# An HGRN2 attention block with a PReLU network behind it: increments as a stage of their own, other banks for two products, and a new order of the stages

## The chip, the cores and the metric

The kernel runs on one core of one Trainium2 chip. The metric is the time of one execution on the device in microseconds (us). A profiled execution has its own time, and its span runs from the first to the last recorded instruction.

## The reference

Four sequences of 768 tokens with eight heads of 48 channels go through a gated linear recurrence; the result, 3072 tokens of 384 channels, goes through a two-layer network with 2048 hidden channels. All is float32.

```python
f = 1.0 / (1.0 + np.exp(-f_logit))
for t in range(S):
    state = f[:, :, t, :, None] * state + np.einsum('bhd,bhe->bhde', k[:, :, t], v[:, :, t])
    y[:, :, t] = np.einsum('bhd,bhde->bhe', q[:, :, t], state)
# (B, H, S, D) -> (B * S, H * D) = x
h = x @ w_in
g = np.maximum(h, 0.0) + alpha * np.minimum(h, 0.0)
out = g @ w_out
```

## The kernel before

The sequence is cut into six chunks of 128 tokens (C), the batch into two pairs (U = 2), which gives twelve steps, `steps = [(bp, c) for c in range(NC) for bp in range(B // U)]`, numbered from zero here. Steps n and n + 2 belong to the same pair; the second needs the state that the first leaves. A chunk is cut into halves of 64 tokens (index `cc`) and blocks of 32 (DB). What is written below holds for steps 2 to 11; steps 0 and 1 have a start of their own.

Each step goes through stages, Python generators that yield between pieces. A piece is what is issued between two yields.

- P, `prepare`, 8 pieces: 1 the loads of f, q, k and v; 2 sigmoid and copies on ScalarE; 3 products of decays on VectorE; 4 copies on ScalarE and two scans; 5 to 7 scaled keys and queries on VectorE, among them `keys`, which ends with a 32x32 block transpose of the keys into `kt` (L422); 8 copies of scaled queries into A on ScalarE (L460).
- S and T, `scores` for u = 0 and 1, 4 pieces each: products of 32-token blocks on PE into `pairs[u]` (L579), masked copies into `ad` on VectorE (L588), products again, masked copies again (L598).
- K, `keys_moved`: 16 DMAs from `kt` to `ksn` that finish the transpose, eight issued by SP and eight by POOL (L470). M, `landed`: one ScalarE copy from `ksn` back into `kt` (L478).
- O, `carry`, 4 pieces: off products, between the two blocks of a half (PE, L511); their copies into A (ScalarE, L518); state increments, keys by values (PE, L542), which read `kt`; `moved(0)`, which decays the state and adds the first half's increments (VectorE, L552 and L556).
- Y, `attend`, 4 pieces: 1 and 2 copies of `ad` into A (ScalarE, L622); 3 the attention output, A by values and state (PE, L633); 4 its copies into `y` (ScalarE, L640), `moved(1)`, and ten DMAs from `y` to `xT`, spread over SP, ScalarE's and POOL's queues (L663). `y` and `ksn` share one buffer.
- n, `network`, 13 pieces. Pieces 1 to 8 are the first layer: each is six matmuls of 128x256 into a bank `ph` (L678), a negated relu on ScalarE (L683) and two VectorE operations into `gate` (L685); after the fourth and eighth, four VectorE sums into S (L764). The second layer is a 2x2 block product with seven block products instead of eight, each eight matmuls of 128x192 (L717): piece 9 is pa and pb, 10 pc and pd, 11 the second part of pa and of pc, 12 pe, three VectorE additions (L721) and the store of o1, 13 the last addition and the store of o0. pa, pc, pd and pe name the accumulators.
- a, w, b, g, W, i, j, X occur at the start only: weights, idle matmuls, and the handing over of banks.

On PE, VectorE, ScalarE and SP (SyncE, which only issues DMAs) instructions stand in the order in which the pieces are called; this order is a hand-held list, a start string and a round that repeats. A word `T:2` calls two pieces, a plus sign means the next step, and n runs for the step before:

```python
USUAL = "T:2 S:2 n:3 M n T:2 S n P+ S n P+ n:3 Y O P+ O:2 Y O n P+ Y:2 P+ n:3 P+:3 K+"
```

In round n the network of step n - 1 runs while scores, off products, increments and output of step n and the preparation of step n + 1 are set between its pieces.

PSUM has eight banks of 512 float32 columns. Four belong to `pairs` (two tiles of two banks): scores go to both, then off products and output to `pairs[0]`, increments to `pairs[1]`. The other four are handed to the network as a pool of four buffers, taken in turn by `bank`.

Of the kernel before, what the change touches and what calls it, by code (L numbers as in the profile page):

```python
# [8 lines left out]
F32 = mybir.dt.float32  # L9
# [5 lines left out]
AF = mybir.ActivationFunctionType  # L15
# [5 lines left out]

U = 2
CH = 64
NC2 = C // CH
# [4 lines left out]

BEGUN = 5  # L30
START = (
# [7 lines left out]
)  # L39
USUAL = "T:2 S:2 n:3 M n T:2 S n P+ S n P+ n:3 Y O P+ O:2 Y O n P+ Y:2 P+ n:3 P+:3 K+"  # L40

LOOSE = ("a", "w", "b", "g", "W", "i", "j", "X")

# [17 lines left out]
def kernel(  # L61
# [66 lines left out]
    def banks_of_network():  # L128

        early_ps.close()  # L130
        net["pool"] = ctx.enter_context(tc.tile_pool(name="psn", bufs=4, space=bass.MemoryType.PSUM))
        yield

    def bank(name):
        return net["pool"].tile([128, 512], F32, tag="net", name=name)

# [131 lines left out]
    def halves(cc):  # L268

        return slice(CH * cc, CH * cc + CH), slice(CH * (1 - cc), CH * (1 - cc) + D)  # L270

    def prepare(bp, c, x):

# [16 lines left out]

        for cc in range(NC2):
            t_, _ = halves(cc)
            loads.dma_start(out=vs[bp][t_, cc, :, 0:DM], in_=v[b0:b0 + U, c, t_].rearrange("u t d -> t u d"))
        yield
# [123 lines left out]
        def keys():  # L418
            nc.vector.tensor_tensor(ks[:, :, 0], kh, f32[:, 1:G:2].broadcast_to((128, GC, DB)), ALU.mult)
            if c:  # L420
                kt = x["kt"] = late["kt"].tile([128, W], F32, tag="kt", name=f"kt_{i}")
                nc.vector.transpose(kt, ks.rearrange("p g s t -> p (g s t)"))  # L422

# [38 lines left out]
        yield  # L462

    def keys_moved(bp, c, x):
        kt, i = x["kt"], f"{bp}_{c}"
        ksn = x["ksn"] = work.tile([128, U, HP * 128], F32, tag="ksn", name=f"ksn_{i}", bufs=1)
        for a in range(4):
            n = min(32, D - 32 * (a % 2))
            for b in range(NJ):
                (nc.gpsimd if a % 2 else nc.sync).dma_start(  # L470
                    out=ksn[32 * b:32 * (b + 1)].rearrange("p u (h x) -> p (u h) x", h=HP)[:, :, 32 * a:32 * a + n],
                    in_=kt[32 * a:32 * (a + 1)].rearrange("p (g b x) -> p g b x", b=NJ, x=32)[:, :, b, 0:n])
        yield
# [8 lines left out]
    def carry(bp, c, x):  # L482

        i = f"{bp}_{c}"
        home = more if (bp, c) == steps[0] else pairs
        off = home[0]
        if not c:
# [14 lines left out]
            yield  # L502
        q3, ks, kh, f64 = (x[n] for n in ("q3", "ks", "kh", "f64"))
        for u in range(U):
            for hp in range(HP):
                a = (u * HP + hp) * NC2
                h_ = slice(64 * (hp % 2), 64 * (hp % 2) + 2 * DB)
                o = (u * HP + hp) // 2 * 2 * DB
                for par in range(2):
                    r_ = rows(par)  # L510
                    nc.tensor.matmul(off[h_, par, o:o + 2 * DB], lhsT=kh[r_, a:a + 2].rearrange("p c s -> p (c s)"),  # L511
                                     rhs=q3[r_, a:a + 2, 2], start=True, stop=True)
        yield
        for cc in range(NC2):
            s_ = slice(CH * cc, CH * cc + DB)
            for e in range(2):
                of = off[64 * e + DB * cc:64 * e + DB * (cc + 1), :, 0:U * HP * DB]
                nc.scalar.copy(A[s_].rearrange("p u (r h e) t -> p r u h e t", r=2, e=2)[:, :, :, :, e, CH * cc + DB:CH * (cc + 1)],  # L518
                               of.rearrange("p r (u h c t) -> p r u h c t", u=U, h=HP // 2, c=NC2)[:, :, :, :, cc])

# [12 lines left out]
        yield  # L533
        pd = home[1]
        ksn = x["ksn"]
        for u in range(U):
            for hp in range(HP):
                for cc in range(NC2):
                    for par in range(2):
                        o = (u * HP + hp) * D  # L540
                        s_ = halves(cc)[0]
                        nc.tensor.matmul(pd[rows(par), cc, o:o + D],  # L542
                                         lhsT=ksn[s_, u, hp * 128 + 64 * par:hp * 128 + 64 * par + D],
                                         rhs=vs[bp][s_, cc, u, (2 * hp + par) * D:(2 * hp + par + 1) * D], start=True, stop=True)

        def moved(cc):
# [6 lines left out]
            for par in range(2):  # L553
                now = pd[rows(par), cc, 0:U * HP * D].rearrange("p (u h e) -> p u h e", u=U, e=D)
# [62 lines left out]
    def attend(bp, c, x):  # L617
# [7 lines left out]

        py = (more if (bp, c) == steps[0] else pairs)[0]
        for u in range(U):
            for hp in range(HP):
                for cc in range(NC2):
                    for par in range(2):  # L630
                        hd = 2 * hp + par
                        o = hp * C + CH * cc
                        nc.tensor.matmul(py[64 * par:64 * par + 64, u, o:o + CH],  # L633
                                         lhsT=vs[bp][:, cc, u, hd * D:hd * D + 64],
# [4 lines left out]
        for u in range(U):  # L639
            nc.scalar.copy(y[:, u].rearrange("p h t -> p (h t)"), py[:, u])  # L640
        if c < NC - 1:
            x["moved"](1)
        xT = x["T"] = work.tile([128, NK, T], F32, tag="xT", name=f"xT_{i}")
        if not (bp or c):

            yield
            for kt in range(NK):
                b = bank(f"xt{kt}_{i}")
                these = [hp for hp in range(HP) if 2 * D * hp < 128 * (kt + 1) and 2 * D * (hp + 1) > 128 * kt]
# [19 lines left out]
    def network(bp, c, x):  # L669
        i = f"{bp}_{c}"  # L670
        xT = x["T"]
        plain = (bp, c) == steps[0]
        for f in range(NH):
            ph = bank(f"ph{f}_{i}")
            tiles = (2 * f, 2 * f + 1) if plain else (f, f + NH)
# [19 lines left out]
        if plain:  # L695
            po = [bank(f"po{u}_{i}") for u in range(U)]
            for n, (f, u) in enumerate([(f, u) for f in range(NF) for u in range(U)]):
# [17 lines left out]
        def product(to, of, by, more=False):  # L715
            for f in range(NH):
                nc.tensor.matmul(to[:, 0:DH], lhsT=of(f), rhs=by(f), start=(f == 0 and not more), stop=(f == NH - 1),  # L717
                                 skip_group_check=True)

        def plus(to, of, by, scale=UP):  # L720
            nc.vector.scalar_tensor_tensor(to, of[:, 0:DH], scale, by, ALU.mult, ALU.add)  # L721

        o0, o1 = (work.tile([128, DM], F32, tag="o", name=f"o{u}_{i}") for u in range(U))
        kept, u2, u3 = (late["C"][:, n] for n in range(3))
        pa, pb = (bank(f"p{n}_{i}") for n in "ab")
        product(pa, a11, b11)
        product(pb, a22, t4)
        nc.scalar.activation(kept, pa[:, 0:DH], AF.Copy, scale=UP)
        yield
        pc, pd = (bank(f"p{n}_{i}") for n in "cd")  # L730
# [6 lines left out]
        plus(o0[:, DH:DM], pd, u2)  # L737
        nc.scalar.activation(o0[:, 0:DH], pa[:, 0:DH], AF.Copy, scale=UP)
        if (bp, c) == steps[-1]:
            store(0, o0, slice(0, DH))  # L740
        yield
        pe = bank(f"pe_{i}")
        product(pe, s4, b22)
# [22 lines left out]
    def halves_of_w_out():  # L766
# [4 lines left out]
        late["S"] = pool.tile([128, 4, NH, C], F32, tag="S", name="S")  # L771
        late["C"] = pool.tile([128, 3, DH], F32, tag="C", name="Csum")
        for n in ("t2", "t3", "t4"):
# [35 lines left out]
    with tc.manual_schedule(engines={mybir.EngineType.PE, mybir.EngineType.DVE, mybir.EngineType.Activation,  # L809
                                     mybir.EngineType.SP}):  # L810
        run = {}
        for n, step in enumerate(steps):
            x = {}
            for key, stage_ in zip("POYKMn", (prepare, carry, attend, keys_moved, landed, network)):
                run[key, n] = stage_(*step, x)
# [58 lines left out]
```

## Time and profile before

| | us |
|---|---|
| median of three runs | 603.27 |
| the three runs | 602.59 to 605.02 |
| the profiled execution | 602.63 |
| its span | 600.8 |
| TensorE clock granted, as a share of full speed | 1.00 |

PE is TensorE's matmuls, PEld its weight loads, DVE VectorE, ACT ScalarE, POOL GpSimd, SP SyncE; a q behind the name (SPq) means the queue of an engine's DMA issues. In groups of instructions `xT<-y` is output and input; L717 is a line of the kernel; `x352` a count. A float32 matmul shows as two instructions, so counts are twice the matmuls that are written. Behind the bar stand busy time in us and the mean of one in ns, then idle time of the engine before them and what ended it. In the chain of waits a row is start, length, work. In a timeline a row is start, length, engine, line, operation, with idle time before it in brackets.

### The profile page before, as it was taken

The numbers are of one execution on the slowest core, as the hardware profiler recorded it, in microseconds if no ns is written. First come the engines' busy times: TensorE is split into PE (matmuls) and PEld (weight loads), VectorE is DVE, ScalarE is ACT, GpSimd is POOL, SyncE is SP. The second block draws the span as 40 slices with busy tenths as digits, with TensorE's granted clock in tenths as the row PEclk, the third lists the DMA queues.
The fourth block names the chain that finished last, engine by engine and source line by source line (L and its number), as shares of the span: only waits on it lengthen the run. The fifth ranks groups of instructions, "written<-read, shape, count | busy, mean of one in ns | idle before, by whom it ended". The sixth has DMA issues, their size and how long they took to land.

```text
span 600.8 us, 18092 instructions
## 1 busy us (share of the span) xinstructions
PE 575.7 (96%) x7760; PEld 516.4 (86%) x7760; DVE 495.3 (82%) x998; ACT 246.6 (41%) x430; POOL 85.1 (14%) x162
## 2 busy tenths in 40 slices
PE   2489999999999999999999999999999999999997
PEld 1378667898899899899899889899899899899997
DVE  7989999997888769988997897997997997891351
ACT  5679951711452441550550451352343344232110
POOL 9210014013003003002100300300300300300000
PEclk9999999999999999999999999999999999999999
DMA  8778836025006303402501602601601511201000
GB/s 261 258 215 299 250 85 125 1 71 108 2 2 176 37 2 63 151 1 62 151 2 55 158 3 55 159 2 41 161 12 31 156 29 27 55 1 29 27 1 27
DMA packets 52880, 50.36 MB, mean 84 GB/s; under 512 B 26720, under 2 KB 43360, under 8 KB 52800
## 3 DMA queue, kind: packets, MB, share of 16 engines
q1 hardware_dynamic: 42784, 37.46, 22.3%
q0 software_dynamic: 5504, 9.90, 6.6%
q10 hardware_dynamic: 4512, 1.85, 1.3%
q8 instruction: 61, 1.00, 0.7%
q14 instruction: 19, 0.16, 0.1%
HBM read 36.21 MB, written 4.72 MB: 68 GB/s over the span
## 4 chain that ended last, share of the span: by engine, by line
PE 87%; DVE 8%; ACT 2%; POOL 1%; issue 1%; DVEq 0%; ACTq 0%; POOLq 0%
PE ph L678 39%; PE pc L717 10%; PE pa L717 10%; PE pair L579 6%; PE pe L717 5%; PE pd L717 5%; PE pb L717 5%; PE pair L633 3%; DVE gate L685 1%; PE pair L542 1%; DVE w_out_sb L248 1%; PE pair L511 1%; PE po L698 1%; DVE ad L598 1%; POOL mhalf L183 1%
## 5 line engine op out<-in xcount | busy, mean ns | idle before, releaser
L678 PE MATMUL ph<-xT,w_in_sb 128*128 128x256 f32 x1152 | 255.3, 381 | 0.6 <-DVE w_in_sb L248 0.6
L678 PEld LDWEIGHTS ph<-xT,w_in_sb 128*128 128x128 f32 x1152 | 216.9, 190 | 32.7 <-issue 2.2
L683 ACT ACTIVATE neg<-ph 128x512 f32<-128x512 f32 x96 | 56.1, 593 | 124.6 <-PE ph L678 81.1
L685 DVE SCALAR_TENSOR_TENSOR gate<-neg,om,ph 128x256 f32<-128x256 f32 x192 | 81.7, 478 | 27.9 <-ACT neg L683 27.8
L717 PE MATMUL pa<-w_out_sb,gate 128*128 128x192 f32 x352 | 62.7, 330 | 0.4 <-DVE gate L685 0.4
L717 PE MATMUL pc<-t,S 128*128 128x192 f32 x352 | 61.6, 328 | 0.0
L460 ACT COPY A<-q 48x512 f32<-48x512 f32 x44 | 27.1, 617 | 83.7 <-DVE q L408 83.2
L717 PEld LDWEIGHTS pa<-w_out_sb,gate 128*128 128x128 f32 x352 | 57.3, 190 | 2.4 <-DVE gate L685 1.0
L470 POOL DMA_DIRECT2D ksn<-kt x80 | 46.1, 584 | 85.6 <-DVE kt L422 61.4
L717 PEld LDWEIGHTS pc<-t,S 128*128 128x128 f32 x352 | 57.4, 190 | 0.4
L663 POOL DMA_DIRECT2D xT<-y x22 | 11.8, 543 | 289.2 <-ACT y L640 289.1
L598 DVE COPY_PREDICATED ad<-mquad,pair 128x224 f32<-128x224 int32 (+6 forms) x140 | 41.7, 298 | 4.1
L588 DVE COPY_PREDICATED ad<-mraw,pair 128x256 f32<-128x256 int32 (+1 forms) x96 | 41.2, 453 | 4.2 <-PE pair L579 0.9
L364 DVE TENSOR_TENSOR us<-us,fs 128x768 f32<-128x768 f32 (+5 forms) x60 | 36.9, 615 | 1.1
L764 DVE TENSOR_TENSOR S<-gate 128x512 f32<-128x512 f32 x44 | 30.2, 687 | 0.8
L717 PE MATMUL pe<-w_out_sb,S 128*128 128x192 f32 x176 | 30.5, 327 | 0.0
L717 PE MATMUL pb<-t,gate 128*128 128x192 f32 x176 | 30.4, 326 | 0.0
L717 PE MATMUL pd<-w_out_sb,S 128*128 128x192 f32 x176 | 30.4, 326 | 0.0
L552 DVE TENSOR_TENSOR vs<-vs,f 48x768 f32<-48x768 f32 x20 | 19.1, 953 | 13.4 <-PE pair L633 12.0
L622 ACT COPY A<-ad 32x512 f32<-32x512 f32 x48 | 29.4, 613 | 0.6
L640 ACT COPY y<-pair 128x512 f32<-128x512 f32 x22 | 11.8, 589 | 43.1 <-PE pair L633 43.1
L717 PEld LDWEIGHTS pe<-w_out_sb,S 128*128 128x128 f32 x176 | 28.8, 190 | 0.1
(125 smaller groups left out, 720.2 us busy)
## 6 DMA issues: line engine op xcount, KB each, us to landing
w_out_raw<-in_w_out SPq DMA_DIRECT2D x8, 767.8 KB, 6.7
w_in_raw<-in_w_in SPq DMA_DIRECT2D x8, 767.2 KB, 9.1
out<-o SPq DMA_DIRECT2D x23, 192.0 KB, 1.9
q<-in_qT SPq DMA_DIRECT2D x8, 512.0 KB, 5.1
k<-in_kT SPq DMA_DIRECT2D x8, 512.0 KB, 7.2
f<-in_fT SPq DMA_DIRECT2D x7, 512.0 KB, 4.0
vs<-in_v SPq DMA_DIRECT2D x16, 192.0 KB
ksn<-kt SPq DMA_DIRECT2D x80, 32.0 KB, 2.2
```

Of the source, the lines that this page charges most:

```text
L364: nc.vector.tensor_tensor(us[:, :, UO[m]:UO[m] + 4 * n].rearrange("p g (i r) -> p g i r", r=4), us[:, :, skip:skip + 4 * n].rearrange("p g ...
L460: nc.scalar.copy(A[halves(cc)[1], :, par * HP:(par + 1) * HP, CH * cc:CH * (cc + 1)], q3[rows(par)].rearrange("p (u h c) s t -> p u h c (s ...
L470: (nc.gpsimd if a % 2 else nc.sync).dma_start(out=ksn[32 * b:32 * (b + 1)].rearrange("p u (h x) -> p (u h) x", h=HP)[:, :, 32 * a:32 * a + n],
L579: nc.tensor.matmul(to[DB * j:DB * (j + 1), par, hp * step + lo:hp * step + hi], lhsT=keys[r_, g * DB:(g + 1) * DB], rhs=by[r_, g, lo:hi], ...
L588: nc.vector.copy_predicated(adu[:, :, :, d:4], mraw[:, d, :, d:4].bitcast(I32).unsqueeze(1).broadcast_to((128, H, NB, n)), rv[:, :, QO[d]: ...
L598: nc.vector.copy_predicated(ad[:, u, :, :, 4 * m:DB], mquad[:, lo:lo + n].bitcast(I32).unsqueeze(1).unsqueeze(1).broadcast_to((128, 2, HP, ...
L622: nc.scalar.copy(A[s_].rearrange("p u h t -> p (u h) t")[:, :, s_], ad[s_].rearrange("p u r h t -> p (u r h) t"))
L678: nc.tensor.matmul(ph[:, j * T:(j + 1) * T], lhsT=w_in_sb[:, kt, m * 128:(m + 1) * 128], rhs=xT[:, kt], start=(kt == 0 and j == 0), stop=( ...
L683: nc.scalar.activation(neg, phv, AF.Relu, scale=-1.0)
L685: nc.vector.scalar_tensor_tensor(gate[:, m % NH, m // NH], neg[:, j], om[:, m:m + 1], phv[:, j], ALU.mult, ALU.add)
L717: nc.tensor.matmul(to[:, 0:DH], lhsT=of(f), rhs=by(f), start=(f == 0 and not more), stop=(f == NH - 1), skip_group_check=True)
L764: nc.vector.tensor_tensor(to, x_, y_, op)
```

## The change

- FAR = 6: from step 6 on, off products go to two of the network's four banks and the attention output to two others. The pool becomes four fixed tiles, and `roles(n)` gives them in an order that turns with the step.
- The network's second layer uses three banks: pb stands beside pa in one bank, pd beside pc in the next, pe in the third. The value that was kept in `u2` is now kept in o0.
- Increments become a stage of their own, D (`increments`), with 3 pieces: products; for steps from 6 on, a ScalarE copy of the second half's increments into `kept`; `moved(0)`. From step 6 on they write columns 80 to 127 of each head's 128 in `pairs`, which the first score products leave free. O keeps two pieces, off products and copies; from step 6 on there are eight copies instead of four, one for each bank.
- The block transpose of the keys becomes a stage Q (`turned`) from step 6 on.
- Values of steps 5 and later are loaded in the fourth piece of Y two steps before (the same pair), by SP, ahead of the DMAs to `xT`.
- The order is new from the network of step 0 on; the start string reaches one round further (BEGUN 6 instead of 5). The repeated round runs scores and off products of step n + 1 and the preparation of step n + 2 beside the network of step n - 1.

The core of the diff:

```diff
+FAR = 6
-BEGUN = 5
+BEGUN = 6
...
-    "O1 g n0 b O1 P2 g:2 b Y1 g b P2 n0:2 O1 n0 O1 b:3 g:2 O1 g n0 Y1:2 g W:2 P2 n0 Y1 T2 W S2 P2 P3 T2 "
...
+    "O1 g n0 b O1 P2 g:2 b Y1 g b P2 n0:2 O1 n0 O1 b:3 g:2 O1 g n0 Y1:2 g W:2 P2 n0 Y1 T2 P2:2 S2 T2 W:2 "
+    "P3 S2 P3 n0 P3 n1 K2 n1:2 M2 T2 S2:2 T2 n1:3 W n1 Y2 O2 D2:2 O2 Y2 D2 P3 n1:2 P3 Y2:2 P3 n1:2 S3:2 "
+    "T3:2 P3 n1:2 P4 P3 K3 S3 T3 n1 P4 T3 n2 S3 P4 Y3 n2 M3 n2:2 Y3 O3 D3 P4 D3:2 O3 n2:3 Y3 P4 n2:2 P4 "
+    "Y3 n2 T4 S4 P4 T4 P5 n2 P4 P5 n2 K4 S4 T4 n2 T4 S4:2 P5 M4 n3 P5 Y4 n3 D4:2 O4 n3 P5 n3:3 Y4 O4 D4 "
+    "n3:2 Y4:2 n3 P5 T5 P5 S5 P6 n3 P6 K5 T5 S5 P6 n3 T5 S5 n3 T5 n3 S5 P6 M5 n4 P5 n4 D5 Y5:2 D5:2 P6 O5 "
+    "n4:2 O5 n4 P6 Y5 n4 Y5 n4:3 S6 P6 T6 O6 Q6 P6 S6 T6 P7:2 K6 n4 S6 P7 T6 O6 T6 S6 P7:2 n4 M6 n4:2 P7 "
+    "Y6 P7 Y6 "
 )
-USUAL = "T:2 S:2 n:3 M n T:2 S n P+ S n P+ n:3 Y O P+ O:2 Y O n P+ Y:2 P+ n:3 P+:3 K+"
+USUAL = "D T+ S+ D n P++ n D n:3 T+ n S+ n:2 Y:2 n T+:2 P++ S+ Q+ P+ O+:2 n P++ S+ P++ n:2 P++ K+ M+ n Y+:2 P++:2"
...
+    def roles(n):
+        r = (0, 1, 2, 3)
+        for _ in range(n):
+            r = (r[3], r[2], r[0], r[1])
+        return [net[x] for x in r]
...
+    def values(bp, c):
+        for cc in range(NC2):
+            t_, _ = halves(cc)
+            (nc.gpsimd if 0 < steps.index((bp, c)) < 5 else nc.sync).dma_start(
+                out=vs[bp][t_, cc, :, 0:DM], in_=v[U * bp:U * bp + U, c, t_].rearrange("u t d -> t u d"))
...
+    def turned(bp, c, x):
+        x["kt"] = late["kt"].tile([128, W], F32, tag="kt", name=f"kt_{bp}_{c}")
+        nc.vector.transpose(x["kt"], x["ks"].rearrange("p g s t -> p (g s t)"))
+        yield
...
-        off = home[0]
+        ahead = steps.index((bp, c))
+        off = [home[0][:, par] for par in range(2)] if ahead < FAR else roles(ahead - 2)[2:4]
...
+        if not c:
+            yield from increments(bp, c, x)
+
+    def increments(bp, c, x):
...
+        def spare(cc, r_):
+            if ahead < FAR:
+                return (pairs if ahead else more)[1][r_, cc, 0:U * HP * D].rearrange("p (u h e) -> p u h e", u=U, e=D)
+            return pairs[cc][r_].rearrange("p u (h x) -> p u h x", h=HP)[:, :, :, QW:QW + D]
...
+        if c:
+            for par in range(2 if ahead >= FAR else 0):
+                nc.scalar.copy(kept[rows(par)], spare(1, rows(par)))
+            yield
         moved(0)
         yield
...
-        py = (more if (bp, c) == steps[0] else pairs)[0]
+        py = [(pairs if ahead else more)[0][:, u] for u in range(U)] if ahead < FAR else roles(ahead - 1)[0:2]
...
         if c < NC - 1:
             x["moved"](1)
+        if 5 <= ahead + 2 < len(steps):
+            values(bp, c + 1)
...
-            ph = bank(f"ph{f}_{i}")
+            ph = part[f % 4]
...
+        pa, pc, pe = (b[:, 0:DH] for b in part[0:3])
+        pb, pd = (b[:, DH:DM] for b in part[0:2])
         product(pa, a11, b11)
-        product(pb, a22, t4)
+        product(pb, a22, t4, more=True)
...
         product(pc, s2, t2)
-        product(pd, s1, t1)
-        plus(u2, pc, kept)
+        product(pd, s1, t1, more=True)
+        plus(o0[:, DH:DM], pc, kept)
```

More of the change, by code (lines that the diff above doesn't have):

```diff
@@ L130, in banks_of_network @@
         early_ps.close()
-        net["pool"] = ctx.enter_context(tc.tile_pool(name="psn", bufs=4, space=bass.MemoryType.PSUM))
+        psn = ctx.enter_context(tc.tile_pool(name="psn", bufs=1, space=bass.MemoryType.PSUM))
+        for n in range(4):
+            net[n] = psn.tile([128, 512], F32, tag=f"net{n}", name=f"net{n}")
         yield
-    def bank(name):
-        return net["pool"].tile([128, 512], F32, tag="net", name=name)
+    def roles(n):
[3 more added lines that the diff above has]
+        return [net[x] for x in r]
     om = const.tile([128, NF], F32, tag="om", name="om")
@@ L289, in prepare @@
         k = x["k"] = load("k", kT, 1)
-        for cc in range(NC2):
-            t_, _ = halves(cc)
-            loads.dma_start(out=vs[bp][t_, cc, :, 0:DM], in_=v[b0:b0 + U, c, t_].rearrange("u t d -> t u d"))
+        if ahead < 5:
+            values(bp, c)
         yield
@@ L420, in keys @@
             if c:
-                kt = x["kt"] = late["kt"].tile([128, W], F32, tag="kt", name=f"kt_{i}")
-                nc.vector.transpose(kt, ks.rearrange("p g s t -> p (g s t)"))
+                if ahead < FAR:
+                    next(turned(bp, c, x))
         sooner = ahead >= 5
@@ L484, in carry @@
         i = f"{bp}_{c}"
-        home = more if (bp, c) == steps[0] else pairs
-        off = home[0]
+        ahead = steps.index((bp, c))
+        home = more if not ahead else pairs
+        off = [home[0][:, par] for par in range(2)] if ahead < FAR else roles(ahead - 2)[2:4]
         if not c:
@@ L502, in carry @@
             yield
-        q3, ks, kh, f64 = (x[n] for n in ("q3", "ks", "kh", "f64"))
+        q3, ks, kh = (x[n] for n in ("q3", "ks", "kh"))
         for u in range(U):
@@ L510, in carry @@
                     r_ = rows(par)
-                    nc.tensor.matmul(off[h_, par, o:o + 2 * DB], lhsT=kh[r_, a:a + 2].rearrange("p c s -> p (c s)"),
+                    nc.tensor.matmul(off[par][h_, o:o + 2 * DB], lhsT=kh[r_, a:a + 2].rearrange("p c s -> p (c s)"),
                                      rhs=q3[r_, a:a + 2, 2], start=True, stop=True)
@@ L516, in carry @@
             for e in range(2):
-                of = off[64 * e + DB * cc:64 * e + DB * (cc + 1), :, 0:U * HP * DB]
-                nc.scalar.copy(A[s_].rearrange("p u (r h e) t -> p r u h e t", r=2, e=2)[:, :, :, :, e, CH * cc + DB:CH * (cc + 1)],
-                               of.rearrange("p r (u h c t) -> p r u h c t", u=U, h=HP // 2, c=NC2)[:, :, :, :, cc])
+                p_ = slice(64 * e + DB * cc, 64 * e + DB * (cc + 1))
+                to = A[s_].rearrange("p u (r h e) t -> p r u h e t", r=2, e=2)[:, :, :, :, e, CH * cc + DB:CH * (cc + 1)]
+                if ahead < FAR:
+                    nc.scalar.copy(to, home[0][p_, :, 0:U * HP * DB]
+                                   .rearrange("p r (u h c t) -> p r u h c t", u=U, h=HP // 2, c=NC2)[:, :, :, :, cc])
+                else:
+                    for par in range(2):
+                        nc.scalar.copy(to[:, par], off[par][p_, 0:U * HP * DB]
+                                       .rearrange("p (u h c t) -> p u h c t", u=U, h=HP // 2, c=NC2)[:, :, :, cc])
         if not c:
@@ L533, in carry @@
         yield
-        pd = home[1]
-        ksn = x["ksn"]
+        if not c:
+            yield from increments(bp, c, x)
+    def increments(bp, c, x):
+        i = f"{bp}_{c}"
+        ahead = steps.index((bp, c))
+        ksn, f64 = x["ksn"], x["f64"]
+        def spare(cc, r_):
+            if ahead < FAR:
+                return (pairs if ahead else more)[1][r_, cc, 0:U * HP * D].rearrange("p (u h e) -> p u h e", u=U, e=D)
+            return pairs[cc][r_].rearrange("p u (h x) -> p u h x", h=HP)[:, :, :, QW:QW + D]
         for u in range(U):
@@ L539, in carry @@
                     for par in range(2):
-                        o = (u * HP + hp) * D
                         s_ = halves(cc)[0]
-                        nc.tensor.matmul(pd[rows(par), cc, o:o + D],
+                        nc.tensor.matmul(spare(cc, rows(par))[:, u, hp],
                                          lhsT=ksn[s_, u, hp * 128 + 64 * par:hp * 128 + 64 * par + D],
                                          rhs=vs[bp][s_, cc, u, (2 * hp + par) * D:(2 * hp + par + 1) * D], start=True, stop=True)
+        if ahead >= FAR:
+            kept = work.tile([128, U, HP, D], F32, tag="pd", name=f"pd_{i}", bufs=1)
         def moved(cc):
@@ L553, in moved @@
             for par in range(2):
-                now = pd[rows(par), cc, 0:U * HP * D].rearrange("p (u h e) -> p u h e", u=U, e=D)
+                now = kept[rows(par)] if cc and ahead >= FAR else spare(cc, rows(par))
                 if c or cc:
@@ L624, in attend @@
                 yield
-        py = (more if (bp, c) == steps[0] else pairs)[0]
+        ahead = steps.index((bp, c))
+        py = [(pairs if ahead else more)[0][:, u] for u in range(U)] if ahead < FAR else roles(ahead - 1)[0:2]
         for u in range(U):
@@ L632, in attend @@
                         o = hp * C + CH * cc
[L633 removed]
+                        nc.tensor.matmul(py[u][64 * par:64 * par + 64, o:o + CH],
                                          lhsT=vs[bp][:, cc, u, hd * D:hd * D + 64],
@@ L639, in attend @@
         for u in range(U):
-            nc.scalar.copy(y[:, u].rearrange("p h t -> p (h t)"), py[:, u])
+            nc.scalar.copy(y[:, u].rearrange("p h t -> p (h t)"), py[u])
         if c < NC - 1:
             x["moved"](1)
+        if 5 <= ahead + 2 < len(steps):
+            values(bp, c + 1)
         xT = x["T"] = work.tile([128, NK, T], F32, tag="xT", name=f"xT_{i}")
@@ L647, in attend @@
             for kt in range(NK):
-                b = bank(f"xt{kt}_{i}")
+                b = roles(0)[(2, 3, 1)[kt]]
                 these = [hp for hp in range(HP) if 2 * D * hp < 128 * (kt + 1) and 2 * D * (hp + 1) > 128 * kt]
@@ L672, in network @@
         plain = (bp, c) == steps[0]
+        part = roles(steps.index((bp, c)))
         for f in range(NH):
-            ph = bank(f"ph{f}_{i}")
+            ph = part[f % 4]
             tiles = (2 * f, 2 * f + 1) if plain else (f, f + NH)
@@ L695, in network @@
         if plain:
-            po = [bank(f"po{u}_{i}") for u in range(U)]
+            po = part[0:U]
             for n, (f, u) in enumerate([(f, u) for f in range(NF) for u in range(U)]):
@@ L716, in product @@
             for f in range(NH):
-                nc.tensor.matmul(to[:, 0:DH], lhsT=of(f), rhs=by(f), start=(f == 0 and not more), stop=(f == NH - 1),
+                nc.tensor.matmul(to, lhsT=of(f), rhs=by(f), start=(f == 0 and not more), stop=(f == NH - 1),
                                  skip_group_check=True)
         def plus(to, of, by, scale=UP):
-            nc.vector.scalar_tensor_tensor(to, of[:, 0:DH], scale, by, ALU.mult, ALU.add)
+            nc.vector.scalar_tensor_tensor(to, of, scale, by, ALU.mult, ALU.add)
         o0, o1 = (work.tile([128, DM], F32, tag="o", name=f"o{u}_{i}") for u in range(U))
-        kept, u2, u3 = (late["C"][:, n] for n in range(3))
-        pa, pb = (bank(f"p{n}_{i}") for n in "ab")
+        kept, u3 = (late["C"][:, n] for n in range(2))
+        pa, pc, pe = (b[:, 0:DH] for b in part[0:3])
+        pb, pd = (b[:, DH:DM] for b in part[0:2])
         product(pa, a11, b11)
-        product(pb, a22, t4)
-        nc.scalar.activation(kept, pa[:, 0:DH], AF.Copy, scale=UP)
+        product(pb, a22, t4, more=True)
+        nc.scalar.activation(kept, pa, AF.Copy, scale=UP)
         yield
-        pc, pd = (bank(f"p{n}_{i}") for n in "cd")
         product(pc, s2, t2)
-        product(pd, s1, t1)
-        plus(u2, pc, kept)
+        product(pd, s1, t1, more=True)
+        plus(o0[:, DH:DM], pc, kept)
         yield
@@ L736, in network @@
         product(pc, s3, t3, more=True)
-        plus(o0[:, DH:DM], pd, u2)
-        nc.scalar.activation(o0[:, 0:DH], pa[:, 0:DH], AF.Copy, scale=UP)
+        plus(o0[:, DH:DM], pd, o0[:, DH:DM])
+        nc.scalar.activation(o0[:, 0:DH], pa, AF.Copy, scale=UP)
         if (bp, c) == steps[-1]:
@@ L741, in network @@
         yield
-        pe = bank(f"pe_{i}")
         product(pe, s4, b22)
@@ L771, in halves_of_w_out @@
         late["S"] = pool.tile([128, 4, NH, C], F32, tag="S", name="S")
-        late["C"] = pool.tile([128, 3, DH], F32, tag="C", name="Csum")
+        late["C"] = pool.tile([128, 2, DH], F32, tag="C", name="Csum")
         for n in ("t2", "t3", "t4"):
@@ L813 @@
             x = {}
-            for key, stage_ in zip("POYKMn", (prepare, carry, attend, keys_moved, landed, network)):
+            for key, stage_ in zip("POYQKMDn", (prepare, carry, attend, turned, keys_moved, landed, increments, network)):
                 run[key, n] = stage_(*step, x)
```

2 lines of the change are left out of this document (1 added, 1 removed), and 5 rows, old and new, of the table START.

## The prediction

> **What bounds the kernel now.** I read the page's busy shares, then the chain that ended last, cut to one steady round, then the windows by round.
>
> ```profile
> PE 575.7 (96%) x7760; PEld 516.4 (86%) x7760; DVE 495.3 (82%) x998; ACT 246.6 (41%) x430; POOL 85.1 (14%) x162
> ...
> PE 87%; DVE 8%; ACT 2%; POOL 1%; issue 1%; DVEq 0%; ACTq 0%; POOLq 0%
> ```
> ```profile
> 419.46 1.52 PE pair L579 x112
> 420.99 10.60 PE ph L678 x48
> 431.59 1.79 PE pair L579 x123
> ...
> 446.54 2.60 PE pb L717 x16
> ...
> 449.76 0.72 PE pair L542 x64
> 450.48 2.80 PE pc L717 x16
> 453.28 2.60 PE pd L717 x16
> 455.88 2.02 PE pair L633 x64
> 457.89 2.80 PE pa L717 x16
> 460.69 2.60 PE pc L717 x16
> 463.29 2.60 PE pe L717 x16
> ```
> ```profile
> 94.00:139.51 45.51, 45.51 (x567) 41.31 (x571) 43.44 (x85) 15.88 (x30) 6.51 (x11) 1.00 0.33 70
> 139.51:185.16 45.65, 45.65 (x674) 41.55 (x673) 36.62 (x76) 18.27 (x32) 5.94 (x11) 1.00 0.18 38
> 185.16:232.79 47.63, 47.63 (x520) 43.85 (x527) 38.76 (x83) 18.33 (x32) 5.68 (x10) 1.00 0.32 72
> 232.79:279.18 46.39, 46.39 (x632) 42.54 (x639) 40.09 (x83) 17.88 (x32) 5.68 (x10) 1.00 0.26 70
> 325.56:373.07 47.51, 47.10 (x633) 42.49 (x638) 41.29 (x85) 18.00 (x32) 5.70 (x10) 1.00 0.27 69
> 419.46:465.89 46.43, 46.43 (x633) 42.55 (x639) 41.33 (x85) 17.93 (x32) 5.68 (x10) 1.00 0.27 70
> ```
>
> The chain is PE end to end: in a round of 46.4 us every PE piece begins where the last one stopped. The windows (columns: length, PE, PEld, DVE, ACT, POOL) say the same, and that DVE is second with 41.33 of 46.43 us. So a reordering can gain only what PE loses between its pieces, and it loses everything it is made to wait. One round, 325.56 to 373.07, is 1.1 us longer than the steady one.
>
> Of small pieces set into the network's stream there are four in a round: scores, scores, off products with increments, attention output. The product after one takes 2.80 us, a product after a product 2.60: each interruption costs 0.2 us.
>
> **The change, part by part.** *Fewer interruptions.* I counted in both orders, from the second network on, how often small matmuls stand between network pieces: 40 before, 34 after (increments now stand with the first score products, off products with the second). 6 x 0.2 = 1.2 us gained. The number of matmuls is the same.
>
> *The long round* (47.51 against 46.39) lies in the stretch that the new order rearranges: I take its 1.1 us as gained, with nothing gained as the other bound.
>
> *The lead.* From the seventh step scores and preparation run a round further ahead, so by the end of network 4 (steps and networks are counted from zero; 279 us) VectorE must have done one round's worth of that work more.
> ```profile
> L685 DVE SCALAR_TENSOR_TENSOR gate<-neg,om,ph 128x256 f32<-128x256 f32 x192 | 81.7, 478 | 27.9 <-ACT neg L683 27.8
> ...
> L764 DVE TENSOR_TENSOR S<-gate 128x512 f32<-128x512 f32 x44 | 30.2, 687 | 0.8
> ```
> A round's 41.33 us less the gates (81.7 / 12 = 6.8) and the sums (this row is half of them: 2 x 30.2 / 11 = 5.5) is 29.0 us at most. VectorE's idle time in the four windows before 279.18 is 2.07 + 9.03 + 8.87 + 6.30 = 26.3 us. So the cost is between 0 (state updates, also in the 29.0, are not moved) and 2.7 us; I take 1.4.
>
> *Extra ScalarE copies* (eight off copies instead of four, two of the increments kept aside) and the transpose and value loads that are moved: ScalarE is busy 17.93 us of a round, and the value loads go out right after the attention output that frees their place, a round before they are read. Nothing; if that cover failed, the increments would wait for the loads.
>
> *Keys, copy, increments.* Here I see the price. In the repeated order the keys' moves (K) and the copy that collects them (M) stand side by side, behind the network's twelfth piece; the increments (D) open the next round, directly behind the product pe on PE. That gives a line: pc ends, VectorE adds, SP stores o1 (twelfth piece), SP issues its eight key moves, they land, ScalarE copies, PE multiplies. Before, K was followed by M only three network pieces later and by the increments half a round later.
> ```profile
> 422.97 5.21 SPq L470 DMA_DIRECT2D ksn<-kt  x8
> 423.23 4.61 POOL L470 DMA_DIRECT2D ksn<-kt  x8 [9.28 <-DVE kt L422]
> ...
> 428.22 0.60 SPq L284 DMA_DIRECT2D f<-in_fT  x1
> ...
> 433.18 0.83 ACT L478 COPY kt<-ksn 128x768 f32<-128x768 f32 x1
> ...
> 463.35 0.36 DVE L721 SCALAR_TENSOR_TENSOR o<-pd,Csum 128x192 f32<-128x192 f32 x1
> ...
> 464.28 0.35 DVE L721 SCALAR_TENSOR_TENSOR o<-pd,Csum 128x192 f32<-128x192 f32 x1
> 464.65 0.36 SPq L693 DMA_DIRECT2D out<-o  x1
> ```
> ```profile
> ksn<-kt SPq DMA_DIRECT2D x80, 32.0 KB, 2.2
> ```
> SP goes strictly in order: the load of f, free to go long before, leaves at 428.22, just behind the last key move. So in the new order the key moves on SP cannot start when their transpose is done (it stands behind the second score products, with pc, pd, pa and pc, 2.80 + 3 x 2.60 = 10.6 us of PE, still to come, and POOL's eight can go then), but only when o1 is stored. Counted from the end of the second pc: today the store leaves at 464.65 - 463.29 = 1.36. Then 0.36 + 0.05 for the store, 5.21 for eight moves, 1.9 for the last to land (2.2 from its issue; the last issue starts 0.65 before the 5.21 are over, so between 1.55 and 2.2), 0.83 for the copy, 0.1 for two hand-overs: 1.36 + 8.45 = 9.8. PE has only pe meanwhile, 2.60: it stands still for 7.2 us. Behind D on PE wait the next scores and the whole next network; behind M on ScalarE the next A copies and negations, which are not needed before.
>
> *Whether the store is later still.* The products now share banks: pb with pa, pd with pc. The addition that reads pc stands behind pd in program order.
> ```profile
> 448.23 0.63 DVE L314 TENSOR_TENSOR kr<-f 128x256 f32<-128x256 f32 x1
> ...
> 451.31 0.64 DVE L310 TENSOR_TENSOR qd<-qd,f 128x256 f32<-128x256 f32 x1
> ...
> 454.47 0.75 DVE L347 TENSOR_TENSOR_SCAN ps<-fs,ones 128x289 f32<-128x289 f32 x1
> 455.14 0.73 DVE L348 TENSOR_TENSOR_SCAN ss<-fs,ones 128x289 f32<-128x289 f32 x1
> ...
> 457.94 1.07 ACT L640 COPY y<-pair 128x512 f32<-128x512 f32 x2 [3.15 <-PE pair L633]
> ```
> ```profile
> 437.99 2.29 DVE L598 COPY_PREDICATED ad<-mquad,pair 128x224 f32<-128x224 int32 x7
> ```
> The last copies read the output's first half, complete midway through its 2.02 us (455.88 to 457.89), yet began at 457.94, when all of it was written: readers wait for the whole tile. Then the addition on pc waits for pd, and VectorE has from pd's end: that addition 0.27, the next preparation's products (448.23 to 451.95) 3.72, score copies 2.29, two scans (454.47 to 455.87) 1.40, together 7.68. PE needs only 2.60 + 2.60 to the end of pc. VectorE is 2.5 us late, and its four additions (463.35 to 464.63) take 1.28, so the store leaves at 2.48 + 1.28 + 0.08 = 3.84 and the stall is 9.7. Without that wait VectorE starts 2.60 earlier, is in time, and the stall is 7.2. I take 9.7, by the row of the output copies.
>
> The Trainium skill has a rule for it: "PSUM — Partial Sum Buffer", section "PSUM bank collisions raise a hardware error", says that two engines must not touch one bank on the same 32 partitions at once, different columns included. By it the addition on pc waits for pd, and the stall is 9.7; a wait by columns alone would make the sum 10 us smaller.
>
> *The slow start after a stall.*
> ```profile
> 9.27 2.40 PE L579 MATMUL pair<-qd,k 48*32 48x80 f32 x128 [5.59 <-ACT us L341]
> ...
> 30.70 1.53 PE L542 MATMUL more<-vs,ksn 64*48 64x48 f32 x64 [3.46 <-ACT ksn L532]
> ```
> ```profile
> 419.39 1.59 PE L579 MATMUL pair<-qd,k 48*32 48x80 f32 x128
> ...
> 449.58 0.90 PE L542 MATMUL pair<-vs,kt 64*48 64x48 f32 x64
> ```
> After 3 to 6 us of idle PE the increments took 1.53 instead of 0.90 and the first score products 2.40 instead of 1.59. These two groups open the round after each stall: 0.63 + 0.81 = 1.4 us each time.
>
> "TensorE: Matmul & The Clock Gate", section "Part 1: The HAM clock gate" of the Trainium skill, gives half speed for some 3.4 us after such an idle window: 1.7 us a stall, and 1.3 us more in the sum than my rows.
>
> *The sum.* K and M stand side by side in five rounds (for steps 7 to 11; step 6 has an early K). In the last of them no preparation is left, VectorE is in time and the stall 7.2. 4 x 9.7 + 7.2 = 46.0; slow starts 5 x 1.44 = 7.2; lead +1.4; interruptions -1.2; long round -1.1. Together +52.3 us. The profiled execution took 602.63 (span 600.8 and 1.8 around it), so 654.9; the median is 0.64 above it, 603.27, so **655.6**.
>
> **The rivals.** *The light stall:* readers wait by columns, five stalls of 7.2: 36.0 + 7.2 - 0.9 = +42.3, 645.6. For it: VectorE today reads pc while pd is written (but in another bank). Against: the output copies.
>
> *No stall, not slower:* SP issues the key moves as early as POOL does. What follows their start takes 5.21 + 1.9 + 0.83 + 0.1 = 8.0 us, so it decides at the point where SP reaches them more than 8.0 - 2.60 = 5.4 us ahead of the second pc's end. Then only -1.2 - 1.1 + 1.4 remain: 602.4, or 601.0 with the lead hidden. Against it: SP's in-order rows and the store ahead of K.
>
> *VectorE bound, no stall:* the lead doesn't fit, and in the lead-in VectorE also waits up to 2.6 us a network for pd, twice: 602.4 + 5.2 = 607.6. For it: 43.44 of 45.51 busy in one window.
>
> *Crowded landing:* the next loads leave right behind the key moves.
> ```profile
> DMA to landing us min/median/max: 1.7/2.0/6.7
> ```
> At 6.7 instead of 2.2 each stall grows by 4.5: 655.6 + 22.5 = 678.1. For it: the maximum in this row; against: it was one case, the median is 2.0.
>
> **How the numbers follow.** The measurement can tell 0.5% (3.0 us) from no change. Heavy stall 0.56, light stall 0.25, no stall 0.09 (of which 0.03 faster by over 0.5%, if waits that I don't see go too), VectorE bound 0.04, crowded 0.06. Slower is 0.56 + 0.25 + 0.04 + 0.06 = 0.91, same 0.06, faster 0.03. Range: from 638 (light stall, landing at 1.55, half the slow start, no lead: 645.6 - 5 x 0.35 - 5 x 0.72 - 1.4 = 638.9) to 666 (heavy in all five, +2.5; the full lead, +1.3; landing 1.3 us later in each, between the median and the maximum above, +6.5: 665.9). It holds the two stall cases, 0.81.
>
> **What would show it.** Right: PE idle of 7 to 10 us before the increments, put down to the ScalarE copy of kt, in five rounds from about 330 us on; SP's key moves directly behind a store; a round of 54 to 57 us; increments and first scores at 1.5 and 2.4 us; VectorE's addition on pc beginning at pd's end. Wrong: increments that follow pe without idle time; key moves on SP ahead of the store; rounds of 46 us. If the stall is there but the addition begins at pc's end, the light case holds.

## The result, and the profile after

The changed kernel takes 659.48 us in the median of four runs (658.19 to 661.21), the kernel before 602.93 in the runs beside it. The ratio is 1.0932, 95% interval 1.0896 to 1.0969: slower by 56.6 us. The profiled execution took 659.8 us, with a span of 658.0.

The page of the changed kernel, its busy shares and the slices of PE's busy time and of its granted clock:

```profile
PE 584.7 (89%) x7760; PEld 525.1 (80%) x7760; DVE 494.5 (75%) x998; ACT 258.1 (39%) x466; POOL 85.0 (13%) x162
...
PE   2599999999999999999939977994997699599998
...
PEclk9999999999999999999979996997999699799999
```

The number of matmuls is the same as before; PE's share falls from 96% to 89%. Both rows are full up to the middle of the span and then show a dent every third or fourth slice, the clock in the same slices or the next. Who waited, from the waits of the changed kernel (engine and line, what ended the wait, us in total, times, longest), first over the span and then for PE from 300 us on:

```profile
ACT kt L499 <- DMA ksn<-kt: 68.3, 7, 11.7
...
PE pair L582 <- ACT kt L499: 47.6, 6, 9.9
```
```profile
PE pair L582 <- ACT kt L499: 46.3, 5, 9.9
```

From 300 us on PE waits for one thing only, the copy M of the moved keys, five times, ahead of the increments. One stall in order of time, from the timeline of the changed kernel:

```profile
498.45 2.76 PE L767 MATMUL net<-w_out_sb,gate 128*128 128x192 f32 x16
498.73 0.36 DVE L771 SCALAR_TENSOR_TENSOR o<-net,Csum 128x192 f32<-128x192 f32 x1 [2.73 <-ACT us L356]
...
503.65 2.76 PE L767 MATMUL net<-w_out_sb,S 128*128 128x192 f32 x16
...
506.15 0.33 DVE L771 SCALAR_TENSOR_TENSOR o<-net,o 128x192 f32<-128x192 f32 x1
...
507.49 0.36 SPq L743 DMA_DIRECT2D out<-o  x1
508.34 5.19 SPq L491 DMA_DIRECT2D ksn<-kt  x8
...
515.32 0.83 ACT L499 COPY kt<-ksn 128x768 f32<-128x768 f32 x1 [11.56 <-DMA ksn<-kt]
...
516.21 1.53 PE L582 MATMUL pair<-vs,kt 64*48 64x48 f32 x64 [9.79 <-ACT kt L499]
517.67 2.41 PE L625 MATMUL pair<-qd,k 48*32 48x80 f32 x128
520.01 21.52 PE L728 MATMUL net<-xT,w_in_sb 128*128 128x256 f32 x96
```

This is the line that the prediction wrote down. The addition on pc starts at 498.73, when pd is written; the first of the four additions ahead of the store of o1 starts at 506.15, 2.5 us after pe began (503.65); the store leaves at 507.49; eight key moves follow it on SP from 508.34 on and take 5.19 us; the copy starts 1.8 us after the last of them is issued; PE begins 9.79 us after it ran out of work.

The second row puts VectorE's wait down to a ScalarE copy of L356 (498.05 to 498.72) that the addition does not read. In the last of the five rounds that copy is missing, and the same wait is put down to PE:

```profile
556.59 2.76 PE L767 MATMUL net<-w_out_sb,gate 128*128 128x192 f32 x16
556.87 0.36 DVE L771 SCALAR_TENSOR_TENSOR o<-net,Csum 128x192 f32<-128x192 f32 x1 [2.75 <-PE net L767]
```

In both rounds the addition starts 0.28 us after the product behind pd begins: it waits for pd, and the copy only happens to end then.

### The profile page after: what moved, and what is told of

Its sections match the earlier page's. It is cut to its first block, busy times and chain, and to the rows that moved or that the text cites. A ratio compares the mean times of both kernels' runs of the same rounds, so it can differ in the third digit from the quotient of the medians.

```text
span 658.0 us, 18134 instructions
## 1 busy us (share of the span) xinstructions
PE 584.7 (89%) x7760; PEld 525.1 (80%) x7760; DVE 494.5 (75%) x998; ACT 258.1 (39%) x466; POOL 85.0 (13%) x162
## 5 line engine op out<-in xcount | busy, mean ns | idle before, releaser
L728 PE MATMUL net<-xT,w_in_sb 128*128 128x256 f32 x1152 | 258.5, 385 | 1.4 <-DVE w_in_sb L257 1.4
L728 PEld LDWEIGHTS net<-xT,w_in_sb 128*128 128x128 f32 x1152 | 220.3, 193 | 34.0 <-issue 3.4
L735 DVE SCALAR_TENSOR_TENSOR gate<-neg,om,net 128x256 f32<-128x256 f32 x192 | 82.7, 478 | 81.4 <-ACT neg L733 81.1
L733 ACT ACTIVATE neg<-net 128x512 f32<-128x512 f32 x96 | 56.9, 597 | 161.2 <-PE net L728 129.4
L767 PE MATMUL net<-w_out_sb,gate 128*128 128x192 f32 x352 | 61.9, 329 | 0.0
L767 PE MATMUL net<-t,S 128*128 128x192 f32 x352 | 61.5, 328 | 0.0
L767 PE MATMUL net<-w_out_sb,S 128*128 128x192 f32 x352 | 60.9, 326 | 0.0
L767 PEld LDWEIGHTS net<-w_out_sb,gate 128*128 128x128 f32 x352 | 57.3, 190 | 1.1 <-issue 0.2
L767 PEld LDWEIGHTS net<-w_out_sb,S 128*128 128x128 f32 x352 | 57.8, 190 | 0.2 <-issue 0.2
L767 PEld LDWEIGHTS net<-t,S 128*128 128x128 f32 x352 | 57.4, 190 | 0.5
L356 ACT COPY us<-qd 128x256 f32<-128x256 f32 x48 | 28.2, 669 | 16.6 <-DVE qd L325 11.1
```

The costliest lines, as they stand in the source:

```text
L356: nc.scalar.copy(q4[:, :, :, r], qdv[r][:, :, :, 0])
L728: nc.tensor.matmul(ph[:, j * T:(j + 1) * T], lhsT=w_in_sb[:, kt, m * 128:(m + 1) * 128], rhs=xT[:, kt], start=(kt == 0 and j == 0), stop=( ...
L733: nc.scalar.activation(neg, phv, AF.Relu, scale=-1.0)
L735: nc.vector.scalar_tensor_tensor(gate[:, m % NH, m // NH], neg[:, j], om[:, m:m + 1], phv[:, j], ALU.mult, ALU.add)
L767: nc.tensor.matmul(to, lhsT=of(f), rhs=by(f), start=(f == 0 and not more), stop=(f == NH - 1), skip_group_check=True)
```

## The experiments

My theory: SP's order holds the key moves back behind the store of o1, and everything else that is lost is the slow clock after idle PE. Rivals: the copy and the increments stand too close whatever SP does; VectorE is late by its load, not by the wait for a bank; the groups behind a stall wait for data.

**k_early: K alone put elsewhere.**

```diff
-... S+ Q+ P+ O+:2 n P++ S+ P++ n:2 P++ K+ M+ n Y+:2 P++:2"
+... S+ Q+ P+ O+:2 K+ n P++ S+ P++ n:2 P++ M+ n Y+:2 P++:2"
```

> In the repeated round the key moves K are called right after the off copies of the same step, before network piece 10, so that on SP they stand ahead of the store of o1; the copy M stays where it is. SP's order (my theory): the moves leave when the transpose is done, the copy ends some 2 us before pe does, the five stalls (46.3 us of idle PE) and the slow starts behind them are gone; the profiled 659.8 less 46.3 and some 10 is 603, between 600 and 605. Rival, the place of M and D: the copy stands directly ahead of the increments, the stall stays at 3 us or more a round and the time above 618.

Measured: 602.9 us against 603.3 beside it, ratio 0.9993 (0.9980 to 1.0005). One word of the list, put elsewhere, takes back all of the loss that can be measured, with copy and increments as near to each other as in the changed kernel. In its timeline the key moves now leave with the transpose, on SP and POOL together, and the copy ends a microsecond ahead of PE's need:

```profile
459.41 1.25 DVE L482 STREAM_TRANSPOSE kt<-ks 128x1024 f32<-128x1024 f32 x1 [0.57 <-issue]
460.68 5.22 SPq L491 DMA_DIRECT2D ksn<-kt  x8
460.94 4.61 POOL L491 DMA_DIRECT2D ksn<-kt  x8 [8.89 <-DVE kt L482]
469.13 0.83 ACT L499 COPY kt<-ksn 128x768 f32<-128x768 f32 x1 [0.71 <-DMA ksn<-kt]
...
471.00 0.94 PE L582 MATMUL pair<-vs,kt 64*48 64x48 f32 x64
```

So the rest of the change, taken together, gains nothing that can be measured.

**o1_by_act: the list unchanged, the store on another queue.**

```diff
-            nc.sync.dma_start(out=out[t0:t0 + C, d], in_=o[:, d])
+            (nc.scalar if u and 5 <= steps.index((bp, c)) < 10 else nc.sync).dma_start(out=out[t0:t0 + C, d], in_=o[:, d])
```

> The list of pieces is that of the changed kernel, K still behind piece 12, but the store of o1 is issued by ScalarE's queue instead of SP's in the networks of steps 5 to 9. SP's order: nothing is left ahead of the key moves on SP that waits, they leave with the transpose, no stall of PE before the increments, 600 to 606. Rival, the position of K in the list counts by itself (or the moves wait for something else than the store): stalls of 7 to 10 us stay, about 660.

Measured: 623.61 us in one run, between the two. The timeline of the last of the five rounds:

```profile
526.38 5.18 SPq L491 DMA_DIRECT2D ksn<-kt  x8
...
535.59 0.35 ACTq L743 DMA_DIRECT2D out<-o  x1
536.52 0.83 ACT L499 COPY kt<-ksn 128x768 f32<-128x768 f32 x1 [4.56 <-DVE o L771]
...
537.40 0.94 PE L582 MATMUL pair<-vs,kt 64*48 64x48 f32 x64 [0.62 <-ACT kt L499]
```

K has kept its place in the list, and its moves leave at 526.38, with the transpose: the position by itself does nothing, the waiting store ahead on the same queue does. But now the copy M stands behind that store on ScalarE's queue, and both wait for the same additions. The stalls are 2.9 us four times and 0.62 once instead of 9.6 to 9.9 and 7.3. My 600 to 606 missed that: I had moved the blocking instruction ahead of another link of the same line.

**prep_first: VectorE's next products ahead of the addition on pc.**

```diff
-... O+:2 n P++ S+ P++ n:2 P++ K+ M+ n Y+:2 P++:2"
+... O+:2 P++ n S+ P++ n:2 P++ K+ M+ n Y+:2 P++:2"
```

> VectorE's products of the next preparation (P, piece 3) are called before network piece 10 instead of after it, so VectorE does them while it would wait for pd. The wait for the bank (my theory): the additions for o1 come 2.5 us sooner in the four rounds that have a preparation, their stalls go from 9.7 to about 7.2, the time from 659.8 to about 650. Rival, VectorE's lateness is just its load: stalls of 9.7 and 660 stay.

Measured: 651.41 us in one run. The increments in its timeline:

```profile
337.38 1.53 PE L582 MATMUL pair<-vs,kt 64*48 64x48 f32 x64 [7.64 <-ACT kt L499]
394.62 1.53 PE L582 MATMUL pair<-vs,kt 64*48 64x48 f32 x64 [7.32 <-ACT kt L499]
450.65 1.53 PE L582 MATMUL pair<-vs,kt 64*48 64x48 f32 x64 [7.41 <-ACT kt L499]
507.78 1.54 PE L582 MATMUL pair<-vs,kt 64*48 64x48 f32 x64 [7.52 <-ACT kt L499]
563.43 1.53 PE L582 MATMUL pair<-vs,kt 64*48 64x48 f32 x64 [7.28 <-ACT kt L499]
```

The four heavy stalls are now nearly as short as the last, though VectorE has the same work: the wait for pd made it late. In the round of the fourth row the first of the four additions begins 0.20 us after pe (497.69 and 497.49) instead of 2.50. That the whole time met my 650 is in part luck: the stalls are 9.1 us shorter in sum, but from the increments of step 6 to the end the kernel takes 649.6 - 282.84 = 366.8 us, only 6.4 less than the changed kernel. In two rounds the clock stayed low for longer, and their first layers took 23.09 and 22.78 us; the other 2 us lie ahead of that stretch, where the two programs are the same.

**k_all_sp: a dose.** SP issues all sixteen key moves of steps 7 to 11.

```diff
-                (nc.gpsimd if a % 2 else nc.sync).dma_start(
+                (nc.gpsimd if a % 2 and steps.index((bp, c)) <= FAR else nc.sync).dma_start(
```

> For steps 7 to 11 SP issues all sixteen key moves instead of eight. The length of SP's issue (my theory): eight more at 0.65 us lie on the line from the store to the increments, the five stalls grow by 5.2 us each, to 14.9 (12.5 in the last), and 659.8 becomes some 686. Rival, the stall ends with something else than SP's last move (ScalarE's queue, a landing that takes long for another reason): growth under 2 us a stall, time under 670.

Measured: 686.64 us in one run. PE's idle time before the increments is 15.52, 14.57, 14.58, 14.52 and 12.23 us. Eight more issues, about 5 us more in each stall: the moves' issue time lies on the line in full.

```profile
410.47 1.53 PE L582 MATMUL pair<-vs,kt 64*48 64x48 f32 x64 [14.57 <-ACT kt L499]
...
598.00 1.53 PE L582 MATMUL pair<-vs,kt 64*48 64x48 f32 x64 [12.23 <-ACT kt L499]
```

**warm and warm_full: PE kept busy in the stall.** In warm, 16 matmuls on constants; in warm_full, 23 or 17. They add work that nothing reads.

```diff
+        for _ in range((0, 23, 17)[(ahead > FAR) + (ahead == len(steps) - 1)]):
+            nc.tensor.matmul(roles(ahead - 1)[0][:, 0:256], lhsT=ones[:, 0:128], rhs=ones[:, 0:256], start=True, stop=True)
```

> Sixteen matmuls of 128x256 on constants, some 6.9 us, stand on PE ahead of the increments of steps 7 to 11, into a bank that is free then; they add work that the result doesn't use. Idle PE makes PE slow: the increments take 0.90 instead of 1.53 us and the first score products 1.59 instead of 2.41, the first layer behind them about 21.0 instead of 21.7, and the time falls by 7 to 10 us to about 651. Rival, these groups wait for their own data after a stall: they stay at 1.53 and 2.41 and the time at 660.

> The matmuls on constants ahead of the increments now fill the whole stall: 23 of them (9.9 us) for steps 7 to 10, 17 (7.3 us) for step 11. Slow clock after idle PE: granted clock 1.00 throughout, increments near 0.9 us, first score products near 1.6, first layer near 20.9; the stretch from the increments of step 6 to the end, 373.2 us in the changed kernel, falls by the 10.3 us that the slow starts cost, to about 363. Rival, the groups behind a stall wait for data as well: 1.5 and 2.4 us stay and the stretch is 373.

Measured: 662.99 and 660.2 us, one run each: no gain, against what I expected. The windows (columns: length, busy times, granted clock, DMA) start at the increments: first the changed kernel behind a stall, then one round of warm_full. PE's timelines of that round and of an earlier one of warm_full follow:

```profile
341.30:346.10 4.80, 4.79 (x194) 4.33 (x195) 1.66 (x6) 3.27 (x6) 0.00 (x0) 0.50 0.59 210
346.10:347.10 1.00, 1.00 (x4) 0.80 (x3) 0.00 (x0) 0.00 (x0) 0.00 (x0) 0.53 0.57 127
347.10:357.10 10.00, 10.00 (x48) 8.81 (x47) 4.67 (x9) 2.13 (x4) 0.00 (x0) 1.00 0.11 41
```
```profile
462.07:467.07 5.00, 5.00 (x205) 4.54 (x205) 1.39 (x4) 3.09 (x6) 0.00 (x0) 1.00 0.77 244
```
```profile
462.07 0.94 PE L585 MATMUL pair<-vs,kt 64*48 64x48 f32 x64
462.93 1.60 PE L628 MATMUL pair<-qd,k 48*32 48x80 f32 x128
464.46 20.99 PE L731 MATMUL net<-xT,w_in_sb 128*128 128x256 f32 x96
```
```profile
347.46 0.78 PE L628 MATMUL pair<-qd,k 48*32 48x80 f32 x28 [2.98 <-issue]
```

The mechanism is as expected: without the filling the granted clock is 0.50 for some 5 us behind the stall; with it, in the round shown, it is 1.00, and the increments take 0.94, the scores 1.60, the first layer 20.99 us instead of 1.53, 2.41 and 21.5 or more. That rules out the wait for data. The gain shows round by round: from increments to increments two rounds of warm_full take 56.27 and 56.26 us, the same two of the changed kernel 58.29 and 58.26.

But the longer program met new waits of PE that the profile puts down to nothing ("issue"): 2.98 and 1.67 us inside first score products and 1.14 us inside off products, in warm 2.49, 3.24 and 1.01 us. The first of them let the clock drop again, from 347.2 to 350.6 us; its round, in which 1.14 us of the stall were left unfilled as well, takes 63.50 us instead of 58.35. The round with the 1.67 us gains nothing (55.67 against 55.63). That is where the gain went. In warm, 16 matmuls left 2.7 to 3.2 us of idle PE in four rounds, and the clock still fell: in three of them within 1.6 us of PE's restart, in the fourth behind the wait of 3.24 us.

No run tests what these waits are, but the traces have a hint. The profile lists a DMA queue of the kind "instruction" (q8) with packets of 16 KB, and each of the six waits ends 1.3 to 1.5 us after the end of such a packet (345.96 and 347.46 us in the first). Most likely PE stood without its next instructions; that is argued, not shown, and most such packets pass without a wait.

**k_best.** K early as above, K of step 4 ahead of network 2's piece 12, increments behind the first score products.

```diff
-    "... P4 T4 P5 n2 P4 P5 n2 K4 S4 T4 ..."
+    "... P4 T4 P5 n2 P4 P5 K4 n2 S4 T4 ..."
-USUAL = "D T+ S+ D n ..."
+USUAL = "T+ S+ D:2 n ..."
```

> K ahead of piece 10 as in the run before; besides, K of step 4 is called ahead of network 2's piece 12, and in the repeated round the increments stand behind the first score products instead of ahead of them. SP's order holds in the start as well: the wait of about 1 us before the increments of step 4 is gone; the increments take 0.72 instead of 0.86 us behind other small products, five or six times: 602.9 becomes 601.0 to 601.5, just below the kernel before. Rival, PE is full and the start's scatter decides: 602.5 to 603.5, no difference.

Measured: 601.24 us against 603.32, ratio 0.9969 (0.9950 to 0.9987): 0.3% shorter than the kernel before. Against k_early no difference is shown, since the intervals of the two ratios overlap and the two were not run side by side. The wait before the increments of step 4 (1.36 us in the changed kernel, 0.95 in k_early) is gone. The other part did nothing: from their start to the next group's, the increments take 0.86 us behind the scores as they did ahead of them. My 601.0 to 601.5 counted on both parts, so that the time met it is in part luck. The chain of waits of k_best there:

```profile
330.12 1.53 PE pair L625 x114
331.64 0.86 PE pair L582 x64
332.51 20.92 PE net L728 x96
```

## Why the prediction was right, point by point

**The line from the store to the increments:** right. Predicted stalls 9.7 four times and 7.2; measured in the changed kernel:

```profile
341.31 1.53 PE L582 MATMUL pair<-vs,kt 64*48 64x48 f32 x64 [9.91 <-ACT kt L499]
...
399.66 1.53 PE L582 MATMUL pair<-vs,kt 64*48 64x48 f32 x64 [9.60 <-ACT kt L499]
...
571.84 1.53 PE L582 MATMUL pair<-vs,kt 64*48 64x48 f32 x64 [7.28 <-ACT kt L499]
```

With the two between them (9.69 and 9.79) that is 46.3 against 46.0. The store left 507.49 - 503.65 = 3.84 us after pe began, predicted 3.84 after pc's end; the light case would have been 1.36. One term was off: from the store to the first key move 0.85 us passed, predicted 0.41. The others make up for most of it: PE worked 2.77 us on pe, predicted 2.60, and the landing took 1.8 instead of 1.9.

**The wait for the bank:** right; in all five rounds the addition on pc starts 0.27 or 0.28 us after the product behind pd begins, and prep_first shows that this wait made VectorE late. The rule of "PSUM — Partial Sum Buffer" in the Trainium skill, section "PSUM bank collisions raise a hardware error", agrees with this case, as far as the kernel's own waits go. Each tile of the network is one bank here, so no run tells a wait for the bank from a wait for the tile.

**The slow start:** the mechanism was right, the size too small. The increments took 0.6 us more in five rounds and the first scores 0.8 in four, as the rows of before had it (6.2 against 7.2 summed, since step 11 has no scores behind it). What I left out is the first layer: behind the five restarts the clock stays at 0.50 for 5.7, 5.4, 5.2, 4.9 and 3.9 us, longer than these groups last, and the first layer took 21.52 to 22.18 us instead of the 20.99 of k_early, 4.1 us in all. Together 10.3 against 7.2. The 3.4 us at half speed of "TensorE: Matmul & The Clock Gate" in the Trainium skill, section "Part 1: The HAM clock gate", would have given 8.5. The length shows in this case as a unit: the stretches at 0.50, which begin while PE is still idle, last 10.2 us four times and 6.8 us in the last round, three and two times 3.4.

**Interruptions:** wrong in size: predicted -1.2, measured about -0.3, if each of the six rounds gained what a steady one did. A steady round of k_early takes 46.34 us, of before 46.39.

```profile
378.33:424.67 46.34, 46.34 (x626) 42.61 (x625) 40.96 (x86) 20.11 (x39) 5.68 (x10) 1.00 0.27 70
```

From start to start, the network's pieces became 0.20 us shorter a round, which is the one interruption that I counted. But off products and increments, 1.34 us side by side before, take 0.63 + 0.86 = 1.49 apart. I had counted what a big product loses behind a small one, and not what the increments gain behind the off products. Not every small neighbour does it: behind the scores, in k_best, they take 0.86 as well.

**The long round:** predicted -1.1. Behind the increments of step 6 the longest round of k_early takes 46.80 us, where before had one of 47.51, so at least 0.7 us of it was gained.

**The lead:** predicted +1.4 through VectorE; from 95 to 331 us PE waited for VectorE nowhere. PE lost 1.36 us there, before the increments of step 4, for the reason of the five stalls: K4 stands behind network 2's piece 12, and in k_best, where it stands ahead of it, the wait is gone. I had missed that one; that the two errors nearly cancel is luck.

**The sum.** Seen from the increments of step 6 to the end, the changed kernel takes 658.0 - 284.83 = 373.2 us and k_early 601.7 - 285.19 = 316.5. The difference of 56.7 is 46.3 of idle time and 10.3 of slow clock: next to nothing is left over. 655.6 was 3.9 us low, by the slow start (3.1) and the interruptions (0.9). The round of 54 to 57 us that was named as a sign was too short even by the prediction's own terms, 46.4 + 9.7 + 1.4 = 57.5; the three rounds between long stalls took 58.3.

```profile
284.83 0.94 PE L582 MATMUL pair<-vs,kt 64*48 64x48 f32 x64
```
```profile
285.19 0.94 PE L582 MATMUL pair<-vs,kt 64*48 64x48 f32 x64
```

## What to carry to other kernels

In an order written by hand, go through the queue of every engine that issues DMAs: a store that waits for the last result of a round held back the DMAs behind it on SP here, and among them can be the one that the next round begins with. Count such a line from its last wait to the engine that needs it, with the issue time of each DMA in it. Moving the store to another queue helps only if nothing of the same line stands behind it there.

Two accumulators in one bank joined their readers in this kernel: the first was read only when the second was written. That made four of the five stalls 2.3 to 2.6 us longer than the last.

## What I had not expected of the hardware

In the changed kernel the granted clock stayed at 0.50 for 3.9 to 5.7 us after PE's restart behind stalls of 7.3 to 9.9 us, and in one round of prep_first for 8.1 us behind 7.64 us. About 3 us of idle PE can be enough to lower it: in o1_by_act it fell behind three of four stalls of 2.9 us, for 3.4 us each time, and not behind the other one. Packing small matmuls beside big ones gained 0.05 us a round out of 0.2, because the increments, taken from the off products, take longer. In a program with more matmuls PE stood still for up to 3.24 us amid a group, each time until 1.3 to 1.5 us after an instruction packet had landed.
